# Attention scores in three steps instead of four, with zero-padded K pieces, and a gate value spread by TensorE

## Chip, cores, metric

One Trainium2 chip, one core. The metric is the device time of one execution in microseconds (us); smaller is better. Times are medians of several executions. The profile gives the start and length of nearly every instruction of one of them.

## The reference, cut to what matters

There are 8 sentences of 576 positions. Each goes through causal attention with 8 heads of width 64 and a forget gate that makes old keys count less; then each whole sentence goes through one of 8 experts, chosen by a gate.

```python
scores = (q @ k.T) / sqrt(64)
cum    = cumsum(log(clip(f, 1e-4, 1)))
scores = where(causal, -1e9, scores + cum[:, None] - cum[None, :])
x      = softmax(scores) @ v                     # 8 sentences x 576 x 512
e      = argmax(mean(x, over positions) @ w_gate)    # one expert per sentence
gate   = softmax(mean(x) @ w_gate)[e]
out    = gate * (relu(x @ w1[e]) @ w2[e])        # 512 -> 1024 -> 512
```

## The kernel before

Work comes in 16 groups (g0 to g15) of four heads, two per sentence, and 8 experts (b=0 to 7). A group is: transposes of q and k on DVE, score matmuls, exponentials on ACT, causal masks on GpSimd, products with V on TensorE ("PV"), normalisation on ACT and DVE. An expert is: gate, request for the weights W1 and W2, H (16 pieces of four matmuls), relu, O, eviction, store.

The score columns of a group were cut in four steps. Half a step is two heads, in a tile of two PSUM banks; there are two such tiles, so a step of four heads fills both, and the next step has to wait until the exponentials have read them.

```python
STEPS = (((0, 0, 448, 0),),                        # (K chunk, first q, last q, column)
         ((1, 128, 576, 0),),
         ((2, 256, 576, 0), (4, 512, 576, 320)),
         ((3, 384, 576, 0), (0, 448, 576, 192)))
...
def expo(g, s, halves):
    e = E[od.slot(("e", g))][s]
    for n in halves:
        nc.scalar.activation(e[:, 2*n:2*n+2, :], PS_S[...][:, :, 0:WIDTH[s]], AF.Exp, scale=0.125)
...
def gate6(op, b):                                  # one number to 128 partitions, by a transfer
    nc.sync.dma_start(GATE[i], ROW[i])
```

The order of the instructions on each engine is not written by hand. A small program in the kernel (`Order`) plays the run through once with assumed durations, picks at each moment the ready operation of the best priority, and emits it. After that the order is fixed: each engine works through its own list and waits at the head of the list, even where something later in it would be ready. Where it has nothing for TensorE, it emits filler matmuls that compute nothing. This matters below.

```python
HOP = 0.12                    # assumed time for an engine to see another one's result, us
...
st = od.add(f"S{tag}", "PE", {448: .41, 384: .37, 320: .31}[n], ..., after=..., takes=(("s", (g, s, x)),))
hm = od.add(f"H{b}{j}{half}", "PE", .49, ..., after=[ld if b else quarters[j // 2], g6])
om = od.add(f"O{b}{sb}a", "PE", us, ..., after=list(rel.values()) + ...)   # O waits for all eight h
```

The softmax here doesn't subtract the row's maximum and nothing guards it: scores larger than these inputs give would overflow.

Of the kernel before, what the change touches and what calls it, by code (L numbers as in the profile page):

```python
# [11 lines left out]
P = 128  # L12
# [12 lines left out]
STEPS = (((0, 0, 448, 0),),  # L25
         ((1, 128, 576, 0),),
         ((2, 256, 576, 0), (4, 512, 576, 320)),
         ((3, 384, 576, 0), (0, 448, 576, 192)))
WIDTH = (448, 448, 384, 320)

BLOCKS = ((0, 256, ((0, 0, 0, 256, 0), (1, 1, 128, 256, 0))),
          (256, 576, ((1, 1, 256, 576, 128), (0, 0, 256, 448, 256), (2, 2, 256, 576, 0),
                      (0, 3, 448, 576, 192), (3, 3, 384, 576, 0), (4, 2, 512, 576, 320))))

MAX_SPAN = 72.0

W_LOW, W_HIGH = 8.6e-17, 1.2e16
LN_SCALE = 2.0 ** -3
FILL = 60.0
# [6 lines left out]
LAG = 3  # L46
# [5 lines left out]
LOOK = {1: (0, 0, 0), 2: (0, 1, 2), 3: (1, 0, 2), 4: (1, 0, 2)}  # L52


class Op:
# [3 lines left out]
    def __init__(self, name, engines, us, fn, after=(), prio=0.0, takes=(), gives=(), lands=None, grain=None, runs=0, behind=()):  # L59
        self.name, self.us, self.fn, self.prio = name, us, fn, prio  # L60
        self.engines = engines if isinstance(engines, tuple) else (engines,)
        self.after, self.takes, self.gives, self.lands = list(after), takes, gives, lands
        self.end, self.grain, self.runs = None, grain, runs
        self.behind, self.issued = behind, None
        self.engine = None


class Order:
# [4 lines left out]
    def __init__(self, rings):  # L73
# [6 lines left out]
        self.filler, self.fill_until, self.spare = None, 0.0, 0  # L80
# [22 lines left out]
    def advance(self, now):  # L103


        while self.clock < now - 1e-9:
# [9 lines left out]
            for q in live:  # L116
                if q[0][1] < 1e-6:
                    op = q.pop(0)[3]
                    op.end = self.clock + 0.4
                    self.give(op)  # L120

# [17 lines left out]

    def run(self):  # L140
        left = list(self.ops)
        busy = dict.fromkeys(("PE", "ACT", "DVE", "POOL", "SP"), 0.0)
        now = 0.0
        busy["PE"] = 2.0
        while left:
# [5 lines left out]
            for e, until in busy.items():  # L151
# [4 lines left out]
                for op in left:  # L156
                    if e not in op.engines:
                        continue
                    ready = 0.0
                    for a in op.after:  # L160
                        if a.end is None:
                            ready = None
                            break
                        ready = max(ready, a.end + (0.0 if a.engine == e and a.lands is None else self.HOP))
                    for a in op.behind:
                        if a.issued is None:
                            ready = None
                        elif ready is not None:
                            ready = max(ready, a.issued)
                    if ready is None:  # L170
                        continue
# [13 lines left out]
            if best is None and self.filler is not None and now < self.fill_until and busy["PE"] <= now + 1e-9:  # L185
# [9 lines left out]
            if best is None:  # L195
                assert horizon is not None, (self.held, [o.name for o in left if all(a.end is not None for a in o.after)])
# [3 lines left out]
            op.engine = e  # L200
            for ring, key in op.takes:
# [4 lines left out]
                if ring in self.turn:  # L206
                    self.turn[ring].pop(0)
            if e == "PE" and self.mode(op) != self.last:
# [11 lines left out]
            left.remove(op)  # L220
# [5 lines left out]
def fast_path(ctx, tc, q, k, v, f, moe_w_gate, moe_w1, moe_w2, out, flag):  # L226
# [16 lines left out]
    KT = [const.tile([P, S], fp32, name=f"kt{i}") for i in range(RINGS["qt"])]  # L243
    VF = [const.tile([P, NCH, NH, D], fp32, name=f"vf{i}") for i in range(RINGS["vf"])]
    VB = [const.tile([P, NCH, 4, D], bf16, name=f"vb{i}") for i in range(RINGS["vb"])]
    E = [[const.tile([P, 4, WIDTH[s]], bf16, name=f"e{s}{i}") for s in range(4)] for i in range(RINGS["e"])]
# [13 lines left out]
    ROW = small("row", [1, P])  # L260
    seen_to = const.tile([P, 1], fp32, name="seen")[64:65, :]
# [5 lines left out]
    span = const.tile([NB * NH, 1], fp32, name="span")  # L267
    mxs = const.tile([1, NB * NH], fp32, name="mxs")
    mx8 = const.tile([1, 8], fp32, name="mx8f")
    WF = const.tile([P, NB, NCH, NH], fp32, name="WF")  # L270
    WB = const.tile([P, NB, NCH, NH], bf16, name="WB")
    wg = const.tile([P, 4, NE], fp32, name="wg")
    ident = const.tile([D, D], fp32, name="identf")
    still = const.tile([P, 512], bf16, name="still")

# [34 lines left out]
    def first(op):  # L310
        nc.scalar.preload_act_table_set("natural_log_exp_and_others")
        nc.sync.dma_start(F, f.rearrange("b h s -> (b h) s"))
        nc.vector.memset(still, 0.0)  # L313
        for t in VB:
            nc.vector.memset(t[0:64, 4, :, :], 0.0)
        nc.vector.memset(WF[0:64, :, 4, :], 0.0)

    loadf = od.add("F", "SP", 0.5, first, prio=-50, lands=0.5, grain=.1)
    idop = od.add("ident", "POOL", 0.8, lambda op: make_identity(nc, ident), prio=-1)
# [9 lines left out]
    last = [loadf]  # L329
    for b in range(NB):  # L330
        for c in range(10 if b < VQ else 5):
# [3 lines left out]
                                   takes=(("vf", b),) if c == 0 else (), lands=(1.4 if c5 < 4 else .7) / (2 if b < VQ else 1), grain=.022, runs=(64 if c5 < 4 else 32) // (2 if b < VQ else 1),  # L335
                                   behind=last if b < VQ else [loads_v[b, c - 1]] if c else [])
# [13 lines left out]
    def cum3(op):  # L350
        nc.vector.tensor_scalar_mul(mid, span, -0.5)
        nc.vector.tensor_tensor_scan(CUM, LOGF, LOGF, mid[:, 0:1], op0=ALU.add, op1=ALU.bypass)
# [13 lines left out]
    def cum6(op):  # L366
        pw = PS_W[od.slot(("bank", "cum"))]
        for w in (WF[:, :, 0:4, :], WF[64:P, :, 4, :]):
            nc.vector.tensor_scalar(w, w, W_LOW, W_HIGH, op0=ALU.max, op1=ALU.min)
        nc.vector.tensor_copy(WB.rearrange("p b c h -> p (b c h)"), WF.rearrange("p b c h -> p (b c h)"))  # L370
# [5 lines left out]
    c2 = od.add("cum2", "ACT", 0.68, cum2, after=[c1], prio=0.5)  # L376
    c3 = od.add("cum3", "DVE", 1.45, cum3, after=[c2], prio=2)
    c4 = od.add("cum4", "PE", 0.8, cum4, after=[c3, idop], prio=0, takes=(("bank", "cum"),))
    c5 = od.add("cum5", "ACT", .7, cum5, after=[c4], prio=0)
    c6 = od.add("cum6", "DVE", 0.9, cum6, after=[c5], prio=0, gives=(("bank", "cum"),))  # L380
# [3 lines left out]
    def to_t(g, j, lo=0, hi=4):  # L384
        raw = RAW[j][od.slot(("raw", g))][32 * lo:32 * hi].bitcast(fp32).rearrange("p (r w) -> p r w", w=32)
        dst = (QT, KT)[j][od.slot(("qt", g))][32 * lo:32 * hi].rearrange("p (t r) -> p r t", r=18)
        nc.vector.transpose(dst, raw)  # L387

    def banks_of(g, s, n):

        i = od.slot(("s", (g, s, n)))
        return [(2 * n + j, PS_S[i][:, j, :]) for j in range(2)]

    def step(g, s, halves):
        i = od.slot(("qt", g))
        kt, qt = KT[i].bitcast(bf16).rearrange("p (t r) -> p t r", r=2), QT[i].bitcast(bf16).rearrange("p (t r) -> p t r", r=2)
        for c, i0, i1, col in STEPS[s]:
            for r in range(2):
                for h, ps in [x for n in halves for x in banks_of(g, s, n)]:
                    nc.tensor.matmul(ps[:, col:col + i1 - i0], kt[32 * h:32 * h + 32, KLO[c]:KLO[c] + P, r],  # L400
                                     qt[32 * h:32 * h + 32, i0:i1, r], start=(r == 0), stop=(r == 1))

    def expo(g, s, halves):
        e = E[od.slot(("e", g))][s]
        for n in halves:
            nc.scalar.activation(e[:, 2 * n:2 * n + 2, :], PS_S[od.slot(("s", (g, s, n)))][:, :, 0:WIDTH[s]], AF.Exp, scale=0.125)  # L406

    def mask(g, s):
        e = E[od.slot(("e", g))][s]
        nc.gpsimd.affine_select(out=e[:, :, 0:128], in_=e[:, :, 0:128], pattern=[[0, 4], [1, 128]],  # L410
                                channel_multiplier=-1, base=0, compare_op=ALU.is_ge, fill=0.0)
        if s == 2:
            nc.gpsimd.affine_select(out=e[:, :, 320:384], in_=e[:, :, 320:384], pattern=[[0, 4], [1, 64]],
                                    channel_multiplier=-1, base=64, compare_op=ALU.is_ge, fill=0.0)
# [444 lines left out]
```

## Time and profile before

| | before |
|---|---|
| time, median | 251.07 us (250.03 to 252.89, three runs; a fourth came with the result) |
| TensorE (PE) busy | 229.7 us, 92% of the profiled span of 250.8 |
| ACT / GpSimd (POOL) / DVE busy | 71% / 51% / 46% |
| share of TensorE in the chain that ended last | 73% |
| first H matmul | 39.3 us |
| last matmul | 244.4 us |

The lines themselves, and the order in which they are read, are in the prediction.

To compare the kernels I use one account that the profile does not give directly. For each pair of successive matmuls in the trace I take the time from start to start and subtract a **price**: columns at 2.4 per ns (shared by four where four strips work side by side, by two in the 64-row O group), 2.5 ns for a matmul of the full array, and the 0.13 us that a change between row strips, column strips and the full array costs; all of these come out of this trace. What is left is a **gap**. From 40 us on, the kernel before has 185.4 us of price and 18.0 us of gaps. 17 of its 256 O matmuls have no record, though; at 0.216 us each their 3.7 us sit among the gaps, so 189.1 and 14.3 are the true sums. Its variants below whose records are complete but for one give 188 to 190 and 14 to 16.

### The profile page before, as it was taken

To read this page: it belongs to the slowest core of one execution; us is meant where nothing else is said; L and a number is where in the kernel's file an instruction comes from. 1 tells how busy PE (TensorE), PEld (TensorE's weight loads), DVE (VectorE), ACT (ScalarE), POOL (GpSimd) and SP (SyncE) were. 2 spreads that over 40 slices of the span, in tenths; PEclk is the share of its full clock that TensorE was granted. 3 is DMA by queue.
4 is the path that set the end of the run, shared out by engine and by line. 5 is a ranking of instruction groups with operands and counts; after the bars stand their busy time and mean duration, and the time that the engine had idled before them with its cause. 6 is when DMAs were issued, how large, how long until landed. Compare 5 with 4: busy or idle time off the path is not lost.

```text
span 250.8 us, 8039 instructions
## 1 busy us (share of the span) xinstructions
PE 229.7 (92%) x3304; PEld 146.2 (58%) x3325; DVE 115.4 (46%) x305; ACT 177.2 (71%) x313; POOL 127.0 (51%) x197
## 2 busy tenths in 40 slices
PE   6799997999889999799999999899998999999990
PEld 2333734674366846567458755586586656957840
DVE  3892882667533941278136942694146342200000
ACT  3466846897799968849779874896488787855820
POOL 6046739971995546714992649363822872300000
PEclk9657999999999999979999999999999999999996
DMA  6996849999999999990999999999993598299032
GB/s 119 221 221 118 146 73 180 201 207 212 177 220 212 215 204 226 297 213 8 173 219 213 277 218 215 254 227 209 227 278 76 82 232 216 36 212 256 29 121 75
DMA packets 59946, 45.84 MB, mean 183 GB/s; under 512 B 40896, under 2 KB 43968, under 8 KB 59904
## 3 DMA queue, kind: packets, MB, share of 16 engines
q0 software_dynamic: 14848, 26.22, 59.1%
q1 hardware_dynamic: 32576, 15.90, 25.1%
q10 hardware_dynamic: 12480, 3.15, 6.1%
q8 instruction: 28, 0.46, 0.7%
q14 instruction: 14, 0.11, 0.1%
HBM read 62.03 MB, written 9.44 MB: 285 GB/s over the span
## 4 chain that ended last, share of the span: by engine, by line
PE 73%; DMA 7%; issue 6%; POOL 6%; ACT 3%; DVE 2%; POOLq 1%; ACTq 0%; DVEq 0%
PE ps_w L595 24%; PE ps_w L612 20%; PE ps_s L400 12%; PE ps_w L439 11%; PE ps_w L615 3%; PE ps_w L680 3%; DMA out_dram<-otile 3%; DMA w1e<-in_moe_w_dram 2%; ACT e L406 2%; DMA rawq<-in_q_dram 2%; POOL e L410 2%; POOL vb L423 1%; DVE qt L387 1%; POOL rawk L281 1%; PE ps_w L548 1%
## 5 line engine op out<-in xcount | busy, mean ns | idle before, releaser
L406 ACT ACTIVATE e<-ps_s 128x896 bf16<-128x896 f32 (+2 forms) x128 | 100.2, 834 | 28.7 <-PE ps_s L400 27.9
L410 POOL TENSOR_SCALAR_AFFINE_SELECT e<-e 128x512 bf16<-128x512 bf16 x64 | 41.7, 656 | 69.0 <-ACT e L406 68.4
L595 PE MATMUL ps_w<-xT,w1e 128*128 128x288 bf16 x512 | 71.0, 292 | 3.4 <-DVE xT L459 1.9
L595 PEld LDWEIGHTS <-w1e 128*128 128x128 bf16 x512 | 60.5, 139 | 11.5 <-issue 4.9
L612 PE MATMUL ps_w<-w2e,h1T 128*128 128x512 bf16 x239 | 57.5, 380 | 1.9 <-issue 1.4
L400 PE MATMUL ps_s<-qt,kt 32*128 32x448 bf16 (+4 forms) x768 | 42.1, 289 | 5.6 <-ACT e L406 2.8
L459 DVE SCALAR_TENSOR_TENSOR xT<-ps_w,lr 128x256 bf16<-128x256 f32 (+1 forms) x64 | 26.8, 455 | 37.1 <-ACT lr L449 30.6
L605 ACT ACTIVATE h1T<-ps_w,gate_b 128x288 bf16<-128x288 f32 x77 | 37.4, 499 | 4.9 <-PE ps_w L595 4.7
L612 PEld LDWEIGHTS <-h1T 128*128 128x128 bf16 x256 | 22.8, 98 | 28.5 <-issue 3.6
L603 DVE TENSOR_SCALAR h1T<-ps_w,gate_b 128x288 bf16<-128x288 f32 x51 | 25.3, 505 | 28.6 <-PE ps_w L595 28.2
L400 PEld LDWEIGHTS <-kt 32*128 32x128 bf16 x768 | 17.6, 95 | 27.5 <-issue 21.5
L439 PE MATMUL ps_w<-e,vb 128*32 128x320 bf16 (+4 forms) x1024 | 29.4, 251 | 1.8 <-issue 1.5
L423 POOL TENSOR_TENSOR vb<-vf,WF 128x512 bf16<-128x512 f32 x29 | 30.5, 1053 | 0.3
L387 DVE STREAM_TRANSPOSE kt<-rawk 128x576 f32<-128x576 f32 (+1 forms) x17 | 21.3, 1252 | 19.4 <-DMA rawk<-in_k_dram 16.3
L624 ACT COPY otile<-ps_w 128x512 f32<-128x512 f32 (+1 forms) x25 | 14.0, 560 | 21.9 <-PE ps_w L612 20.9
L439 PEld LDWEIGHTS <-vb 128*32 128x32 bf16 x1024 | 21.3, 97 | 7.0 <-issue 4.7
L387 DVE STREAM_TRANSPOSE qt<-rawq 128x576 f32<-128x576 f32 (+1 forms) x17 | 21.1, 1244 | 0.6 <-DMA rawq<-in_q_dram 0.5
L680 PE MATMUL ps_w<-still 128*128 128x512 bf16 x51 | 17.4, 472 | 2.1 <-DVE still L313 1.4
L622 DVE COPY otile<-ps_w 128x512 f32<-128x512 f32 (+1 forms) x15 | 9.0, 599 | 21.2 <-PE ps_w L612 19.8
L439 PE MATMUL ps_w<-e,WB 128*32 128x192 bf16 (+4 forms) x512 | 17.3, 253 | 0.1
L576 POOL DMA_DIRECT2D w1e<-in_moe_w_dram x14 | 10.2, 731 | 13.1 <-DVE h1T L603 11.4
L444 ACT ACTIVATE lr<-ps_w 128x256 f32<-128x256 f32 (+1 forms) x31 | 12.7, 411 | 4.8 <-PE ps_w L439 4.5
(55 smaller groups left out, 129.4 us busy)
## 6 DMA issues: line engine op xcount, KB each, us to landing
w2e<-in_moe_w_dram POOLq DMA_DIRECT2D x8, 1024.0 KB, 14.2
out_dram<-otile SPq DMA_DIRECT2D x32, 256.0 KB, 7.4
w1e<-in_moe_w_dram POOLq DMA_DIRECT2D x14, 512.0 KB, 7.6
rawk<-in_k_dram POOLq DMA_DIRECT2D x15, 288.0 KB, 7.2
rawq<-in_q_dram POOLq DMA_DIRECT2D x15, 288.0 KB, 8.7
vf<-in_v_dram SPq DMA_DIRECT2D x12, 256.0 KB, 9.3
vf<-in_v_dram ACTq DMA_DIRECT2D x12, 256.0 KB, 12.2
vf<-in_v_dram SPq DMA_DIRECT2D x22, 128.0 KB, 6.0
```

What stands on the lines that cost most here:

```text
L387: nc.vector.transpose(dst, raw)
L400: nc.tensor.matmul(ps[:, col:col + i1 - i0], kt[32 * h:32 * h + 32, KLO[c]:KLO[c] + P, r], qt[32 * h:32 * h + 32, i0:i1, r], start=(r == 0 ...
L406: nc.scalar.activation(e[:, 2 * n:2 * n + 2, :], PS_S[od.slot(("s", (g, s, n)))][:, :, 0:WIDTH[s]], AF.Exp, scale=0.125)
L410: nc.gpsimd.affine_select(out=e[:, :, 0:128], in_=e[:, :, 0:128], pattern=[[0, 4], [1, 128]], channel_multiplier=-1, base=0, compare_op=AL ...
L423: eng.tensor_tensor(vb[:, c, :, :], vf[:, c, h, :], WF[:, b, c, h].unsqueeze(3).to_broadcast([P, 2, 4, D]), op=ALU.mult)
L439: nc.tensor.matmul(ps[32 * h:32 * h + 32, lo - i0:hi - i0], lhs, e[s][:, h, col:col + hi - lo], start=(n == 0), stop=(n == len(parts) - 1) ...
L459: nc.vector.scalar_tensor_tensor(XT[od.slot(("x", b))][:, mm, i0:i1], ps[:, 0:i1 - i0], 1.0 if (g, blk) in ON_DVE else LN_SCALE, LR[od.slo ...
L595: nc.tensor.matmul(ps[:, 0:288], lhs, xT[:, m, 288 * half:288 * half + 288], start=(m == 0), stop=(m == 3))
L603: nc.vector.tensor_scalar(dst, ps[:, 0:288], g[:, 0:1], 0.0, op0=ALU.mult, op1=ALU.max)
L605: nc.scalar.activation(dst, ps[:, 0:288], AF.Relu, scale=g[:, 0:1])
L612: nc.tensor.matmul(ps, h[:, j, P * sb:P * sb + P], r, start=(j == 0), stop=(j == 7))
L680: od.filler = lambda i: nc.tensor.matmul(PS_W[i], still[:, 0:P], still[:, 0:512])
```

## The change

The intent is to spend less TensorE time: one score step and its mode changes less per group, no transfer in the gate's path, and O matmuls that start as soon as half of h is there. Step 2 now holds chunk 2, the upper half of chunk 3 and chunk 4. For that, K gets two extra pieces of which one half is zero, so that a full-height matmul adds a half chunk. The diff, cut to its core:

```diff
-STEPS = (((0, 0, 448, 0),), ((1, 128, 576, 0),),
-         ((2, 256, 576, 0), (4, 512, 576, 320)), ((3, 384, 576, 0), (0, 448, 576, 192)))
+STEPS = (((0, 0, 512, 0),), ((1, 128, 576, 0), (0, 512, 576, 448)),
+         ((2, 256, 576, 0), (None, 384, 512, 320), (3, 448, 576, 384)))
...
+if c is None:                                   # the padded pieces
+    for n in range(2):
+        nc.tensor.matmul(ps[:, col:col+64], kt[row, S+64*n:S+64*n+P, r], qt[row, i0+128*n:i0+128*n+64, r], ...)
...
-nc.sync.dma_start(GATE[i], ROW[i])
+nc.tensor.matmul(ps[:, 0:1], ROW[i], one)       # gate spread by PE
+nc.vector.tensor_copy(GATE[i], ps[:, 0:1])      # (an own piece of the plan)
...
-om = ... after=list(rel.values()) + outs[-1:] + [ld2]
+om = ... after=[x for (j, _), x in rel.items() if j < 4] + outs[-1:] + [ld2]
...
-FILL = 60.0                                     # fillers until 60 us
+FILL = (28.0, 60.0)                             # none before the planned 28 us
-LAG = 3                                         # q, k of group g asked for after V of group g-3 is scaled
+LAG = 2
```

Not shown: a second half-chunk of V to scale, masks that DVE may take (all of groups 2 and 3), V loads that wait for a DVE mark, and other assumed durations in the plan.

## The prediction

> **What bounds the kernel now.** I read the page first (engine shares, slices, chain), then the time-ordered chain, then the timeline of some score steps, then the groups split by shape and the ten-microsecond windows.
>
> ```profile
> PE 229.7 (92%) x3304; PEld 146.2 (58%) x3325; DVE 115.4 (46%) x305; ACT 177.2 (71%) x313; POOL 127.0 (51%) x197
> PE   6799997999889999799999999899998999999990
> PEclk9657999999999999979999999999999999999996
> PE 73%; DMA 7%; issue 6%; POOL 6%; ACT 3%; DVE 2%; POOLq 1%; ACTq 0%; DVEq 0%
> ```
>
> TensorE is busy 92% of the span and carries 73% of the chain, so after the beginning a microsecond of TensorE work is worth about a microsecond. But the digits are dense from the first slices only because of filler matmuls (L680: x51, 17.4 us busy), which compute nothing. The beginning is a latency chain:
>
> ```profile
> 18.06 0.65 PE ps_s L400 x8
> 18.70 2.25 PE ps_w L680 x5
> 20.95 0.76 PE ps_s L400 x6
> 21.74 0.92 ACT e L406
> ...
> 36.19 0.48 POOL w1e L580
> 37.59 6.23 DMA w1e<-in_moe_w_dram
> 43.86 1.40 PE ps_w L595 x10
> ```
>
> Five fillers stand in front of the scores of the second group of four heads (g1) for 2.25 us; the exponentials follow, then masks, PV, the gate, and only then can the expert's W1 be asked for (first request at 35.48 us in the timeline). Dense TensorE work starts when it lands, at 43.86. I count the first 44 us as one account and the rest as another. Up to 44 us TensorE had done real work of about 13.7 us: three score groups, two PV groups, 28 H matmuls, at the warm prices below. So some 30 us of the span are start-up, about 6 us are the last store (last matmul 244.4, end 250.8), and the rest is TensorE work with about 11 us of gaps.
>
> The price of a score step, from start to next start in the timeline:
>
> ```profile
> 45.19 0.58 PE L400 MATMUL ps_s<-qt,kt 32*128 32x448 bf16 x8
> 45.70 2.63 PE L595 MATMUL ps_w<-xT,w1e 128*128 128x288 bf16 x20
> ...
> 50.68 0.54 PE L400 MATMUL ps_s<-qt,kt 32*128 32x320 bf16 x16
> 51.15 1.31 PE L439 MATMUL ps_w<-e,vb 128*32 128x320 bf16 x48
> ...
> 53.97 0.46 PE L400 MATMUL ps_s<-qt,kt 32*128 32x192 bf16 x16
> 54.37 0.35 PE L439 MATMUL ps_w<-e,WB 128*32 128x256 bf16 x8
> ```
>
> 448, 384 and 320 columns cost 0.51, 0.45 to 0.47 and 0.40 us. 64 columns fewer save 0.053 us: two passes at 2.4 columns per ns. What is left is a constant 0.13 us per step, whether it holds 8 matmuls or 16. A group of four steps costs 0.505+0.505+0.453+0.395=1.86 us.
>
> ACT, by shape:
>
> ```profile
> L406 ACT ACTIVATE e<-ps_s 128x896 bf16<-128x896 f32 x64 | 55.2, 913 | 18.3 <-PE ps_s L400 18.0
> L406 ACT ACTIVATE e<-ps_s 128x640 bf16<-128x640 f32 x32 | 20.9, 701 | 3.9 <-PE ps_s L400 3.6 <-DMA vf<-in_v_dram 0.2
> ```
>
> That is 0.83 ns per element and 0.17 us fixed.
>
> **What the Trainium skill says.** "TensorEngine Tiling (Array Packing)", Key Properties, says that changing the tiling mode drains the array. The trace agrees in kind: the 0.13 us that each score step costs beyond its columns appears at every change between row strips, column strips and the full array. "TensorE: Matmul & The Clock Gate", What's actually happening, says the array starts at half clock and is released by activity over a window of about 3.4 us. The trace agrees on the two clocks: the window 10 to 20 us has granted clock 0.50 although TensorE was busy 9.67 of 10 us there, so filling did not buy a warm clock in time. "ScalarE: Activation LUTs", Rules for kernel authors, budgets about 0.3 us and 0.83 ns per element for an activation; the slope agrees, the fixed part here is 0.17, and I use that.
>
> **The change part by part.**
>
> *Scores in three steps.* Columns streamed per group: before 448+448+384+320=1600; after 512+512+(320+64+64+128=576)=1600. Only one 0.13 us constant per group goes: 16 x 0.13 = 2.1 us less. Against it, the zero-padded pieces are two 64-column matmuls in succession on the same row strip, where all others alternate over four strips. If they fully serialize, eight take about five 27 ns slots instead of two: 0.08 us per pass, 0.17 us per group, 2.7 us in all. I take half, 1.3. Net -0.8 us.
>
> *Exponentials.* Before 4x0.913+2x0.807+2x0.701=6.67 us per group as the means of single instructions; in a row they start every 0.81, 0.70 and 0.60 us, 5.84 us. After six of 1024 elements, about 0.92 apart, 5.5 us. Some 5 us of ACT in all, off the path except at the start.
>
> *PV.* Columns stay at 1600; 36 matmuls instead of 32 for each product of a group. Four of 64 columns already take only 27 ns here, so no cost.
>
> *Masks and V.* The e3 mask goes, the second part of e2 goes to DVE for nearly all groups (built order), and groups 2 and 3 have all theirs on DVE. GpSimd's 656 ns masks fall from 64 to about 43 (-14 us), its 418 ns ones go (-7), 14 more V scalings at 0.61 come (+8.5), and seven copies of K. About 10 us less GpSimd; DVE gets these, and 14 more evictions of H, some 15 us, at 46% busy. No direct effect.
>
> *Gate by TensorE.* Eight DMAs go; the one early in the trace took 2.0 us from issue to landing. They were beside the W1 load, whose 512 KB pieces take a median of 7.6 us, so nothing is gained on the path. Eight small fp32 matmuls are added; the four gate matmuls together cost 0.28 us, so I take 0.15 each: +1.2 us.
>
> *O after four of h.* In the last two experts the x16 group of O starts 1.15 us before the next, while at 54.97 it took 1.00: a wait of 0.16 us for the last eviction, in most of 8 experts. Sum -1.0 us.
>
> *The start (not named in the change's title, but in the diff).* No fillers before the planned 28 us (51 or more become 13), V loads start after a DVE mark, behind the first q and k; the flag arithmetic moves off the front; no transpose stands between the gate matmul and its maximum. I walk the chain. V's DMAs begin about 1.4 us later, so first q should land about 1 us earlier than 6.74: first scores near 7 instead of 8.04. The scan and its exponential follow 1 to 1.5 us earlier. g1's raw q and k are asked for about 1.4 us later (they wait behind the first V), so its transposes finish about where they did, 16.4. But its first scores then start there instead of at 20.88, as neither fillers nor late exponentials stand before. At the cold clock the three double steps and the PV between them take about 8 us, so the last exponential of g1 ends near 25.4 instead of 29.3. From there to the last norm took 3.0 us and keeps that. The gate's maximum, held 0.6 us by a transpose (32.41 to 33.66), comes 0.6 us sooner after it. W1 is requested near 31.1 instead of 35.5: -4.4 us. In the built order PV of groups 2 and 3 stands between the first H pieces, where TensorE used to wait for W1 quarters (about 1 us idle at 39.7, 0.5 at 43.3): -1.0.
>
> *Gaps later.* Two stretches stand out:
>
> ```profile
> 60.00:70.00 10.00, 8.35 (x100) 3.50 (x96) 4.75 (x14) 7.58 (x12) 6.72 (x11) 1.00 0.90 183
> 100.00:110.00 10.00, 8.13 (x143) 5.98 (x145) 3.99 (x12) 5.66 (x11) 5.78 (x9) 0.84 1.12 271
> ```
>
> The first is a pile-up of scores on the exponentials while masks wait in GpSimd's queue; the second is DVE's queue held by a K transpose whose transfer is late (6.0 us), followed by a spell of half clock. Fewer steps and less GpSimd work help the first; the second depends on when transfers are issued, and q and k are now asked for one group later, which may hurt. I take -1.5 us.
>
> Sum: -0.8 +1.2 -1.0 -4.4 -1.0 -1.5 = -7.5 us. 251.07-7.5 = 243.5 us.
>
> **Rivals.**
> (1) The start is bound by transfers, not by fillers and exponentials. The DMA share is 1.14 in 10 to 20 us, and the bytes are the same. Then the request for W1 moves by 1 to 2 us only and the time is about 247. For it: the saturated transfers; against it: the fillers lie on the chain at 18.70, and g1's first transpose follows other DVE work at once.
> (2) The clock stays cold longer without fillers, so the PV of g1 and the first H pieces run at half speed. That costs 2 to 3 us: about 246. For it: in the trace the clock rose only after long filling; against it: the later fillers (13) remain.
> (3) Transfers become the bound in the middle: their share is over 1 in most windows, and a shorter lead of q and k loads makes DVE's queue block oftener. Then the start's gain is given back: about 249 or 250.
> (4) GpSimd's queue no longer holds the masks at all, and most of the 11 us of gaps close: about 237.
>
> **Range and chances.** The start is most of it, -2 to -6; gaps -5 to +3; prices of TensorE work within 2. Together 243.5, with 237.5 to 248 eight times in ten. The 2% border is 246.05 and needs about 5 us; the start alone nearly gives it. Faster 0.78, within 0.20, slower 0.02.
>
> **What would show it.** The W1 request near 31 us and dense H work near 36 to 39; score steps of 0.56, 0.56 and 0.61 to 0.78 us; each gate spread at most 0.15 us; the x16 group of O at 1.00 us; TensorE's work after the start shorter by about 1 us and the gaps by 1 to 2. If W1 is requested after 33 us, the walk through the start is wrong; if the total is right but the start is not, the gaps were mis-sized; if the padded step takes over 0.8 us, strip order is the fault.

## The result

| | before | changed |
|---|---|---|
| time, median | 250.55 us (249.38 to 252.89) | 258.92 us (257.70 to 259.64) |
| ratio of fast runs | | 1.032 (1.023 to 1.041): slower |
| first H matmul | 39.3 us | 35.5 us |
| gate matmuls of b=2 | 82.8 us | 91.8 us |
| last matmul | 244.4 us | 251.0 us |

A ratio is the mean time of one kernel's fast runs over that of the other's fast runs of the same rounds, so not quite the ratio of the medians. All runs of both here were fast.

The kernel is 8 us slower; the prediction was 243.5. First the page of the changed kernel (busy time, slices, granted clock, chain by engine):

```profile
PE 225.1 (88%) x3619; PEld 148.6 (58%) x3619; DVE 140.0 (55%) x365; ACT 166.4 (65%) x268; POOL 123.0 (48%) x189
PE   0889888699999987699799999999989898999991
PEclk9999999999999997999999999999999999999999
PE 63%; DMA 18%; DVE 5%; issue 5%; ACT 3%; POOL 2%; POOLq 1%; ACTq 0%; DVEq 0%
```

TensorE has less to do, 225.1 us instead of 229.7, and carries less of the chain, 63% instead of 73%. Transfers took the difference: 18% instead of 7%. The digits 7 and 6 in the middle are the 16th and 17th slice, 96 to 109 us. The chain in order of time shows which transfers (start, length, what):

```profile
19.21 1.92 PE ps_s L454 x16
23.98 3.30 PE ps_w L495 x45
38.09 11.88 DMA rawk<-in_k_dram
...
56.20 12.38 DMA w1e<-in_moe_w_dram
...
94.63 10.77 DMA w1e<-in_moe_w_dram
```

Neither a filler nor a wait for W1 of the first expert is in it now. Instead it holds a load of K for 11.9 us and W1 of the second and third expert for 12.4 and 10.8 us. That the beginning really was shortened is in the timeline of the changed kernel, where the first request for W1 starts at 31.76 us (before: 35.48):

```profile
31.76 4.90 POOL L656 DMA_DIRECT2D w1e<-in_moe_w_dram  x7 [4.32 <-DVE row L627]
```

The score steps, in TensorE's timeline (start, length, what), and ACT's group of exponentials by shape:

```profile
85.49 0.63 PE L454 MATMUL ps_s<-qt,kt 32*128 32x512 bf16 x8
86.05 0.71 PE L495 MATMUL ps_w<-e,WB 128*32 128x320 bf16 x28
...
89.39 0.64 PE L454 MATMUL ps_s<-qt,kt 32*128 32x448 bf16 x16
89.95 1.90 PE L703 MATMUL ps_w<-w2e,h1T 128*128 128x512 bf16 x8
```

```profile
L459 ACT ACTIVATE e<-ps_s 128x1024 bf16<-128x1024 f32 x96 | 93.2, 1020 | 23.2 <-PE ps_s L454 22.2
```

From start to next start the first two steps take 0.56 us each; the third, with the padded pieces, took 0.63 where nothing held it (as at 60.7 and 71.1 us). A group costs 1.75 instead of 1.86 us. ACT's exponentials fell from 100.2 to 93.2 us. So the parts did what they were meant to. The loss is in TensorE's gaps. Ten-microsecond windows (busy PE, PEld, DVE, ACT, POOL; clock; DMA share; GB/s), first of the kernel before, then of the changed one:

```profile
90.00:100.00 10.00, 9.95 (x85) 5.26 (x85) 1.60 (x3) 7.19 (x12) 5.26 (x8) 1.00 1.16 214
120.00:130.00 10.00, 9.79 (x166) 4.94 (x164) 2.42 (x9) 7.10 (x12) 9.81 (x15) 1.00 1.10 190
```

```profile
60.00:70.00 10.00, 9.54 (x96) 4.71 (x95) 2.52 (x5) 7.29 (x9) 1.97 (x4) 1.00 1.12 237
90.00:100.00 10.00, 7.30 (x110) 3.52 (x110) 5.47 (x13) 7.11 (x10) 7.92 (x12) 0.92 1.04 220
100.00:110.00 10.00, 7.53 (x240) 5.01 (x232) 2.77 (x12) 8.07 (x15) 7.07 (x11) 0.91 1.13 210
120.00:130.00 10.00, 8.03 (x189) 4.87 (x186) 3.17 (x11) 7.96 (x12) 9.00 (x14) 1.00 1.12 224
```

The pile-up at 60 to 70 us is gone, as I had hoped (9.54 busy, before 8.35). But in 90 to 100 us TensorE stands still for 2.7 us where before it lost 0.05. The account of gaps from 40 us on, in us, for four of the kernels (two are experiments told below):

```
window        before   f1_b_hop16   changed   g4_a_all
40 to 60        1.1        0.8         5.0       5.2
60 to 80        4.4        3.1         0.7       0.3
80 to 100       0.6        0.4         6.6       5.7
100 to 120      4.5        6.4         4.8       4.5
120 to 140      0.9        1.6         3.5       2.7
140 to 200      5.2        2.2         3.0       2.3
200 to 240      1.4        0.7         4.2       0.6
sum            18.0       15.2        27.7      21.3     (before: 3.7 of it missing records)
price         185.4      189.8       182.7     182.1     (before: 3.7 more)
```

From 40 us on the price fell by 6.4 us (189.1 to 182.7; part of that is work that now lies before 40 us) and the gaps grew by 13.4 us (14.3 to 27.7). Together +7.0, which is the 6.6 us by which the last matmul is later, within 0.4. The question is what the 13 us of gaps are waits for. The longest stretch, in TensorE's timeline of the changed kernel (brackets: idle before it, and what ended the idle time):

```profile
94.19 0.38 PE L631 MATMUL ps_w<-one,row 1*128 1x1 f32 x2 [0.46 <-DVE row L627]
94.84 0.40 PE L454 MATMUL ps_s<-qt,kt 32*128 32x512 bf16 x2 [0.27 <-ACT e L459]
95.75 0.62 PE L454 MATMUL ps_s<-qt,kt 32*128 32x512 bf16 x6 [0.51 <-ACT e L459]
97.28 0.37 PE L454 MATMUL ps_s<-qt,kt 32*128 32x448 bf16 x2 [0.90 <-ACT e L459]
...
103.20 0.34 PE L686 MATMUL ps_w<-xT,w1e 128*128 128x288 bf16 x1
105.44 0.59 PE L686 MATMUL ps_w<-xT,w1e 128*128 128x288 bf16 x3 [1.90 <-DMA w1e<-in_moe_w_dram]
```

Three kinds of waits follow each other: the gate spread holds the queue until DVE has its row, the score steps stand behind exponentials of 1024 elements, and H stands behind W1. Four suspects come from here: the gate, the exponentials, the weights, and the masks and V work (the added V scaling on GpSimd ended when PV went on at 128.7 us, and was taken for what it waited for; the next lines speak against that).

There is a fourth kind, and no experiment was aimed at it. Some pauses of TensorE carry no wait in the profile; they are marked "issue":

```profile
46.99 0.51 PE L495 MATMUL ps_w<-e,vb 128*32 128x256 bf16 x15 [1.94 <-issue]
128.71 0.46 PE L495 MATMUL ps_w<-e,vb 128*32 128x320 bf16 x18 [1.37 <-issue]
```

A third is at 216.30 us. The three, 5.0 us of gaps together, fall inside a PV product that has already begun. Count TensorE's records from the start of the trace (matmuls, weight loads, and its sequencer's own): work resumes at number 1217, 3777 and 6593, each time 193 past a multiple of 256. And 1.3 to 1.5 us before each resumption a packet of 16 KB has landed on queue q8, which the profile calls "instruction" (the first from 44.6 to 45.5 us). The 20 kept traces hold 56 such pauses of 0.3 us or more after 40 us. Every one ends 1.2 to 1.6 us after such a landing, against 12 of the 217 other gaps of that size, and 54 of them at 193 to 195 past a multiple of 256; the other two are in the trace of before, which misses records.

So TensorE very probably waited for its own next instructions there. These pauses are 5.7 us in the changed kernel and 1.9 in before, that is 3.8 of the 13.4 us by which the gaps grew. In the seven kernels of this study with four-step scores they are 0 to 2.3 us, in the thirteen with three steps 1.8 to 7.7. No run varied them on purpose: why there are more with three steps is open.

### The profile page after: what moved, and what is told of

Its sections match the earlier page's. It is cut to its first block, busy times and chain, and to the rows that moved or that the text cites. A ratio compares the mean times of both kernels' runs of the same rounds, so it can differ in the third digit from the quotient of the medians.

```text
span 256.7 us, 8624 instructions
## 1 busy us (share of the span) xinstructions
PE 225.1 (88%) x3619; PEld 148.6 (58%) x3619; DVE 140.0 (55%) x365; ACT 166.4 (65%) x268; POOL 123.0 (48%) x189
## 4 chain that ended last, share of the span: by engine, by line
PE 63%; DMA 18%; DVE 5%; issue 5%; ACT 3%; POOL 2%; POOLq 1%; ACTq 0%; DVEq 0%
PE ps_w L686 23%; PE ps_w L703 18%; PE ps_w L495 10%; DMA w1e<-in_moe_w_dram 9%; PE ps_s L454 8%; DMA rawk<-in_k_dram 5%; PE ps_w L706 3%; DMA rawq<-in_q_dram 2%; ACT e L459 2%; DMA vf<-in_v_dram 2%; POOL w1e L656 1%; DVE xT L515 1%; DVE qt L431 1%; DVE row L627 1%; PE ps_w L612 1%
## 5 line engine op out<-in xcount | busy, mean ns | idle before, releaser
L459 ACT ACTIVATE e<-ps_s 128x1024 bf16<-128x1024 f32 x96 | 93.2, 1020 | 23.2 <-PE ps_s L454 22.2
L703 PE MATMUL ps_w<-w2e,h1T 128*128 128x512 bf16 x256 | 59.7, 380 | 0.4 <-DVE xT L515 0.3
L454 PE MATMUL ps_s<-qt,kt 32*128 32x512 bf16 (+4 forms) x640 | 42.7, 312 | 13.7 <-DVE mid L391 7.4
L467 POOL TENSOR_SCALAR_AFFINE_SELECT e<-e 128x512 bf16<-128x512 bf16 x43 | 28.3, 662 | 50.3 <-ACT e L459 50.3
L694 DVE TENSOR_SCALAR h1T<-ps_w,gate_b 128x288 bf16<-128x288 f32 x65 | 33.0, 516 | 30.1 <-PE ps_w L686 29.3
L696 ACT ACTIVATE h1T<-ps_w,gate_b 128x288 bf16<-128x288 f32 x63 | 31.2, 502 | 25.1 <-PE ps_w L686 24.8
L495 PE MATMUL ps_w<-e,vb 128*32 128x64 bf16 (+3 forms) x1152 | 32.1, 252 | 4.9 <-issue 4.3
L642 POOL DMA_DIRECT2D w1e<-in_moe_w_dram x14 | 10.2, 733 | 24.3 <-DVE kt L431 11.9
L713 DVE COPY otile<-ps_w 128x512 f32<-128x512 f32 (+1 forms) x14 | 8.6, 615 | 22.5 <-PE ps_w L703 19.9
L495 PE MATMUL ps_w<-e,WB 128*32 128x64 bf16 (+3 forms) x576 | 19.0, 258 | 0.4 <-POOL e L467 0.3
L483 POOL TENSOR_TENSOR vb<-vf,WF 64x256 bf16<-64x256 f32 x28 | 17.4, 621 | 2.2
L495 PEld LDWEIGHTS <-WB 128*32 128x32 bf16 x576 | 11.7, 102 | 8.6 <-issue 6.2
```

What stands on the lines that cost most here:

```text
L454: nc.tensor.matmul(ps[:, col:col + i1 - i0], kt[row, KLO[c]:KLO[c] + P, r], qt[row, i0:i1, r], start=(r == 0), stop=(r == 1))
L459: nc.scalar.activation(e[:, lo:lo + 2, :], banks, AF.Exp, scale=0.125)
L467: nc.gpsimd.affine_select(out=x, in_=x, pattern=[[0, 4], [1, P]], channel_multiplier=-1, base=0, compare_op=ALU.is_ge, fill=0.0)
L483: eng.tensor_tensor(vb[rows, d, :, :], vf[rows, c, h, :], WF[rows, b, c, h].unsqueeze(2).to_broadcast([64, 4, D]), op=ALU.mult)
L495: nc.tensor.matmul(ps[32 * h:32 * h + 32, lo - i0:hi - i0], lhs, e[s][:, h, col:col + hi - lo], start=(n == 0), stop=(n == len(parts) - 1) ...
L694: nc.vector.tensor_scalar(dst, ps[:, 0:288], g[:, 0:1], 0.0, op0=ALU.mult, op1=ALU.max)
```

## The experiments

18 kernels ran. "Changed" and "before" are the two kernels above; before ran in the same rounds each time (medians 251.2 to 252.1 us). Unless said otherwise the results were correct. Runs in a slow state are left out of the ratios.

### One part undone, or one part alone

**e1_lag3**: the lag and its look-ahead entry as before.

```diff
-LAG = 2
+LAG = 3
-LOOK = {1: (0, 0, 0), 2: (0, 1, 2), 3: (1, 0, 2)}
+LOOK = {1: (0, 0, 0), 2: (0, 1, 2), 3: (1, 0, 2), 4: (1, 0, 2)}
```

> The changed kernel, with the q and k loads issued as early as before again (one group earlier, and the fourth look back). Theory A (the gaps in the middle come from q and k asked for too late: scores of group 6 start 8.5 us later than before although the start gained 4 us): 250 to 253 us. Theory B (the gaps come from an order of instructions fixed beforehand from planned durations that the chip does not keep, so one part undone gives back only its own price): 256 to 260 us.

Measured: 262.35 us, ratio 1.039 (1.032 to 1.046). Asking for q and k earlier does not help. The theory that the shorter lag is the loss falls.

**e2_gate_dma**: the gate by a transfer again, order kept.

```diff
-nc.tensor.matmul(ps[:, 0:1], ROW[i], one)
+return
-nc.vector.tensor_copy(GATE[i], ps[:, 0:1])
+nc.sync.dma_start(GATE[i], ROW[i])
```

> The changed kernel with every instruction in the same place, only the gate is spread by a DMA again in place of the TensorE matmul and its eviction. Theory C (the spread matmul stands in TensorE's in-order queue and holds it while it waits for the row: gaps of 0.9 and 1.2 us at it, and 8 x 0.31 us of its own): 254 to 256 us. Theories A and B: only its own price, 2 us, 256 to 257.5 us. If the DMA's landing is late for the evictions of H, the time stays or rises.

Measured: 255.77 us, ratio 1.009 (1.002 to 1.017; one of four runs was slow). The change by the median is 3.2 us, by the ratios (1.032 to 1.009, of 251) 5.6 us. So the gate spread costs some 3 to 6 us. Eight spreads of 0.31 us, start to start with their mode changes, are 2.5 us; the rest is what the queue waits for the row, as at 94.19 above.

**e3_o_all**: O after all eight h again, in the plan.

```diff
-after=[x for (j, _), x in rel.items() if j < 4] + outs[-1:] + [ld2]
+after=list(rel.values()) + outs[-1:] + [ld2]
```

> The changed kernel with O planned after all eight of h again. Theory A and C: a wait of 0.16 us in each of 8 experts comes back, 258 to 260 us. Theory B: the order shifts as a whole, so it may land anywhere from 254 to 262 us.

Measured: 257.71 us, ratio 1.023 (1.016 to 1.030; one of four runs was slow). O after four brings nothing here; undoing it is, if anything, better.

**e4_fill0**: fillers from the start, as before (the plan then also drops its allowance for the cold clock).

```diff
-FILL = (28.0, 60.0)
+FILL = (0.0, 60.0)
```

> The changed kernel with fillers from the start again (and so no planned cold price). If the start's gain (first W1 request 3.7 us earlier) is real and carries to the end, this loses it: 260 to 263 us. If the start does not matter because the transfers of the middle bound the time anyway (as much data has moved at 110 us in both kernels), the time stays within 1 us: 258 to 260.

Measured: 261.12 us, ratio 1.033 (1.025 to 1.041). The median is 2.2 us up, the ratio hardly (1.032). The time lies in the range set for a start whose gain carries to the end, but the ratio does not; at most about 2 us of the 3.8 arrive, and even that is not clear of the scatter.

**e5_b_three**: the kernel before with the three-step scores alone (padded K, masks, second V half), nothing else.

```diff
-STEPS = four steps
+STEPS = three steps, KT with 192 more columns, VB and WB with one more chunk
+again(...), the mask of the padded part on DVE or GpSimd, the second V half-chunk
```

> The kernel before with the three-step scores alone (padded K pieces, seven PV parts, the second mask of the last step on DVE or GpSimd, the extra half scaling of V); gate by DMA, O after eight, loads, fillers and planned durations as before. If the three steps are the loss (scores bunched in double steps wait 0.86 us for exponentials; more V scaling on GpSimd): 256 to 259 us. If they are what the column count says and the loss lies elsewhere: 249 to 252 us.

Measured: 263.32 us, ratio 1.045 (1.036 to 1.055). Its gaps from 40 us on are 29.0 us, 9.5 of them between score steps (before 2.3, changed 6.6). Of these 9.5, 3.0 are two pauses without a recorded wait (64.06 and 116.95 us) and 5.3 are six waits for exponentials; in all the pauses without a wait are 7.7 us here. Its first H is at 41.5 us, later than before. The new scores alone open the gaps.

**e6_a_four**: the changed kernel with the four-step scores of before, everything else kept.

```diff
-STEPS = three steps and all that belongs to them
+STEPS = four steps of before
```

> The changed kernel with the four-step scores of before and everything else of the change. If the three steps are the loss: 250 to 253 us. If the rest is (gate on TensorE, load order, planned durations, start): 257 to 261 us.

Measured: 265.08 us, ratio 1.055 (1.046 to 1.065). It looks as if the other half were guilty too, but the profile says otherwise. TensorE's timeline of this run near the end:

```profile
234.61 0.34 PE L670 MATMUL ps_w<-xT,w1e 128*128 128x288 bf16 x1 [4.06 <-DMA w1e<-in_moe_w_dram]
238.16 1.18 PE L670 MATMUL ps_w<-xT,w1e 128*128 128x288 bf16 x4 [3.21 <-DMA w1e<-in_moe_w_dram]
```

In this order the attention of the last sentence came so late that nothing was left to do while the last expert's weights travelled: 7.3 us idle. So this run is inconclusive about the rest of the change.

### Is it the order as such?

By now every kernel with a fresh order was slower than before. The plan had promised 243.7 us for the changed kernel (that is the end that the order-drawing program reports; for before 247.9), and the chip took 15 us longer. Was before's order just a lucky one?

**f1_b_hop16** and **f2_a_hop11**: only the assumed hop in the plan differs, so that about 100 of some 380 pieces of TensorE work change place.

```diff
-HOP = 0.12
+HOP = 0.16        # f1, in the kernel before
+HOP = 0.11        # f2, in the changed kernel
```

> The kernel before with nothing of the change in it. One number that only the program which fixes the order reads is altered: the assumed time for an engine to see another engine's result, 0.12 us -> 0.16 us. Instructions, sizes, loads and buffers are the same; about 100 of the 388 planned pieces of TensorE work stand in another place. The planned end is 247.2 us (unaltered: 247.9). Theory B (the time of before, 251, belongs to one lucky or selected order, and any fresh order ends 13 to 19 us after its plan, as the changed kernel and four of my variants did): 256 to 263 us. Theory C (before is short because of what it does, and the three-step scores, the two-turn lag, the gate spread and the rest cost the 8 us): 250 to 253 us.

> The changed kernel with the same number altered the other way, 0.12 -> 0.11 us; about 97 of 378 planned pieces of TensorE work move; the planned end is 244.5 us (unaltered: 243.7). Theory B: anywhere in 253 to 264 us, since the order decides and the plan does not tell which order is good. Theory C: within 1% of the changed kernel, 256.5 to 261.5 us.

Measured: f1 253.34 us, ratio 1.005 (0.999 to 1.010); f2 259.35 us, ratio 1.030 (1.023 to 1.037). My theory B fell: a redrawn order of before is as good as before, a redrawn order of the changed kernel as slow as it. Gaps from 40 us on: 15.2 and 28.0 us. In f2 they lie elsewhere than in the changed kernel (8.8 of them at 200 to 220 us), but their sum is the same. So, as far as one redraw of each can tell, the content makes the gaps and the order only places them.

**f3_b_ofour**: before, with O after four alone.

```diff
-om = ... after=list(rel.values()) + outs[-1:] + [ld2]
-on = ... after=[om]
+om = ... after=[x for (j, _), x in rel.items() if j < 4] + outs[-1:] + [ld2]
+on = ... after=[om] + list(rel.values())
```

> The kernel before with the third part of the change alone: O begins when four of the eight h are there. Only 24 of 388 planned pieces of TensorE work move; planned end 247.1 us (before 247.9). My prediction put this part at -1.0 us: 250 to 251 us. Theory B, with few pieces moved: between 249 and 256 us. If it is over 253 us, a small re-draw is already enough to lose the tuned order.

Measured: 252.33 us, ratio 1.004 (0.996 to 1.013). Nothing, as in e3_o_all.

**f4_a_gate**: changed, gate by a transfer, order drawn anew.

```diff
-g6 = od.add(f"g6{b}", "PE", .15, ...)    # and g7 on DVE
+g7 = od.add(f"g6{b}", "SP", .5, ..., lands=.2)
```

> The changed kernel with the gate spread by a small transfer as in before, and the order drawn up anew for it (in the earlier run e2_gate_dma the order was kept). Planned end 250.1 us, 6.4 us later than the plan of the changed kernel. If the plan were a guide to the chip this would be 265 us; if the removed 3 us of the gate spread decide, 255 us as in e2_gate_dma; theory B: anywhere in 253 to 264 us.

Measured: 264.99 us median; two of its four runs were slow (the fast ones 261.15 and 262.90), so no ratio is taken. It is not as good as e2_gate_dma, which has the same instructions in another order. The order does matter within the family, by several us; only it does not explain the step from before to changed.

**g1_b_nofill**: before in its own order, without the fillers before 28 us.

```diff
-self.filler(ok[0][1])
+if now >= 28.0:
+    self.filler(ok[0][1])
```

> The kernel before in its own order, with the filler matmuls that the plan places before 28 us left out (the changed kernel has none there either); nothing else differs. In the trace of before the clock is at 0.50 from 8 to 20 us while fillers run, in the changed kernel it is at 1.00 there and the first H starts 3.8 us sooner. If the fillers are what halves the clock and the start is worth its 3.8 us, the time is 247 to 248.5 us, below both kernels. If the rest of the start's gain came from the three-step scores or other loads, 250 to 252 us. If the fillers did warm the clock, later than 252 us.

Measured: 252.71 us, ratio 1.001 (0.994 to 1.009). A window of before, then the same of this run (third figure from the end in each: the granted clock):

```profile
12.00:16.00 4.00, 3.80 (x25) 1.33 (x23) 3.82 (x9) 2.49 (x5) 0.00 (x0) 0.50 1.24 236
```

```profile
12.00:16.00 4.00, 3.20 (x24) 1.60 (x23) 3.83 (x9) 3.48 (x6) 1.78 (x3) 1.00 1.24 235
```

The first PV starts at 17.3 us instead of 21.6, so the fillers did hold up TensorE. But the gate's matmuls come at 30.9 instead of 32.5 and the first H at 39.2 instead of 39.3: the lead is lost again. One reason stands in the matmuls' own times. Without fillers TensorE ran at half speed for longer: four PV matmuls of 320 columns side by side took 0.26 us up to 28.2 us and 0.13 from 29.0 on, while in before they took 0.13 already at 24.2. The granted clock of 1.00 does not tell this. So the fillers did bring full speed sooner, and held up TensorE meanwhile; the fillers alone are not the start's gain.

### What TensorE waits for

The next kernels remove a suspected wait in the fixed order. All were built to give wrong results on purpose (g2_a_exp still passed the comparison with the reference, as stale exponentials of an earlier group stand in for the missing ones).

**e7_b_light** and **e8_a_light**: from the fourth expert on only a quarter of the weights is loaded, in before and in changed.

```diff
+n = 256 if b > 2 else FH
-dma_start(W1[w]...[:, q], src[:, q])
+dma_start(W1[w]...[:, q, :, 0:n], src[:, q, :, 0:n])
+n = 1024 if b > 2 else 4096                    # W2 likewise
```

> WRONG RESULT ON PURPOSE. The kernel before, every instruction in its place, but the experts' weights of batch elements 3 to 7 loaded to a quarter only (the rest of the buffer keeps old values). If transfers bound the middle: 241 to 246 us. If TensorE and the fixed order do: 248 to 250 us.

> WRONG RESULT ON PURPOSE. The changed kernel with the same cut of weights. If the changed kernel is slower because its transfers crowd (Theory T): it falls as far as to the light kernel before or below it, 240 to 247 us. If it is slower because of its order and its waits between engines (Theory B): it stays about 6 to 8 us above the light kernel before, 252 to 257 us.

Measured: before 251.22 us, ratio 0.998 (0.992 to 1.005); changed 254.05 us, ratio 1.011 (1.005 to 1.017). The kernel before shows no wait for these transfers that is clear of the noise. The changed one gains about 5 us (1.032 to 1.011, of 251). Its profile does not say that TensorE waited for the cut weights: TensorE's larger waits for W1 from 40 us on are 2.8 us in both, here all of it for the third expert, whose load this run leaves whole. What fell are the pauses without a recorded wait, from 5.7 to 1.8 us. That fewer bytes let the instructions come in time is a guess; no run tests it.

**g2_a_exp**: exponentials of 256 instead of 1024 elements from group 4 on.

```diff
-activation(e[:, lo:lo+2, :], banks, AF.Exp, ...)
+w = 128 if g > 3 else 512
+activation(e[:, lo:lo+2, 0:w], banks[:, :, 0:w], AF.Exp, ...)
```

> Wrong result on purpose: the changed kernel in its own order, with each exponential cut from 1024 to 256 elements a partition from group 4 on. Theory X (TensorE's gaps of 0.86 and 1.23 us between score steps, at 94 to 99, 108.7 and 125.6 us of the changed trace, wait for the longer exponentials behind two score tiles): 252 to 255 us. If ScalarE's length is not what is waited for: 257 to 260 us.

Measured: 254.64 us, ratio 1.013 (1.004 to 1.021). The gaps between score steps fall from 6.6 to 1.2 us. The prediction had put the exponentials "off the path except at the start"; they are on it. But look at the stretch from before in TensorE's timeline of this run:

```profile
98.23 1.34 PE L496 MATMUL ps_w<-e,vb 128*32 128x320 bf16 x56
101.15 0.34 PE L687 MATMUL ps_w<-xT,w1e 128*128 128x288 bf16 x1 [1.58 <-DMA w1e<-in_moe_w_dram]
103.32 0.94 PE L687 MATMUL ps_w<-xT,w1e 128*128 128x288 bf16 x3 [1.82 <-DMA w1e<-in_moe_w_dram]
```

TensorE came there sooner, and now waits 3.4 us for W1 instead of 1.9.

**g3_a_pool**: masks of one column, and no second V half, from group 4 on.

```diff
+if g > 3:
+    eng.tensor_copy(x[:, :, 0:1], x[:, :, 0:1]); return
-for rows, c, d in (first half, second half):
+for rows, c, d in (first half, second half)[0:1 if g > 3 else 2]:
```

> Wrong result on purpose: the changed kernel in its own order, with the causal masks cut to one column and the added second half-chunk scaling of V left out from group 4 on. Theory M (PV's gaps of 1.2 to 1.6 us at 128.7 and 216.3 us wait for that added work on GpSimd and for the masks): 254 to 256.5 us. If it is beside the path: 257.5 to 260 us.

Measured: 257.97 us, ratio 1.025 (1.017 to 1.032). At most 2 us. At the PV of 128.7 us the GpSimd work that ended last is gone, yet PV resumes only 0.8 us sooner (127.95), after a pause of 1.5 us, 1.2 us after a packet on q8 landed: it was one of the pauses without a recorded wait, and so was the one at 216.3. Theory M was aimed at the wrong wait.

**g4_a_all**: the four cuts together (exponentials, masks and V, late weights, gate).

> Wrong result on purpose: the two cuts above, the weights of the last five experts loaded to a quarter and the gate spread by a transfer, all together, in the changed kernel's own order. If the waits for these four things are the whole loss, little of it is left and the time is 245 to 248 us, near the 243.5 us that I predicted for a kernel whose gaps do not grow. If over 251 us, something else still holds TensorE.

**h2_b_cut**: its control, the same cuts in before (there is no second V half to cut, and the gate is a transfer anyway).

> Wrong result on purpose, the control for g4_a_all: the kernel before in its own order with the same cuts (exponentials to 256 elements and masks to one column from group 4 on, weights of the last five experts to a quarter; its gate is spread by a transfer anyway). g4_a_all fell 7 us below the changed kernel. If those waits are the change's own, before loses little by the same cuts: 249 to 252 us. If it falls to 245 us or less, such waits are in both kernels and the cuts say nothing of the change.

Measured: g4 251.75 us, ratio 0.998 (0.991 to 1.004); h2 248.44 us, ratio 0.996 (0.985 to 1.006), the medians 2.8 us apart. With the four cuts, the changed kernel is level with the uncut before, 3.4% below its own ratio; before itself hardly gains by the same cuts, 0.4% by ratio and 1.1% by medians. Net of the control the cuts take away 3.0 of the 3.2% by ratios, but only 4.4 of the 8.4 us by medians, so they hold between half and nearly all of the loss. Part of that is work and not waiting: eight gate spreads are 2.5 us of TensorE's time. The pauses without a recorded wait stay at 5.7 us in g4. Alone, the four cuts had taken off 2.2, 2.1, 1.9 and 0.7%, which is 6.9% in sum. So they overlap: where one wait is removed, another with nearly the same end takes its place.

**h1_a_light1**: of the weights of every expert but the first, half of W1 and a quarter of W2 are loaded, and the matmuls read that part.

```diff
-dma_start(W1[w]...[:, q], src[:, q])
+dma_start(W1[w]...[:, q, 0:1], src[:, q, 0:1])
-lhs = w1[:, 2 * (m % 2) + m // 2, j::8]
+lhs = w1[:, m // 2, j::8]                      # W2 likewise
```

> Wrong result on purpose: the changed kernel in its own order; of the weights of every expert but the first, half of W1 and a quarter of W2 are loaded, and the matmuls read the loaded part (e8_a_light did this from the fourth expert on and left the loads of the second and third whole). Theory W: the gaps of about 11 us between 80 and 120 us, which no cut so far has moved (g4_a_all kept 10 of them), hang on the weights of the third expert, requested at 93.9 and landed at 105.4 us. Then the time falls another 3 to 6 us below the 254.0 us of e8_a_light, to 248 to 251 us. If it stays at 253 to 255 us, the wait for these weights is beside the path.

Measured: 255.94 us, ratio 1.023 (1.014 to 1.031). Theory W missed. The wait for W1 at 105 us did go, but the stretch in TensorE's timeline of this run says why that gave nothing:

```profile
95.77 0.62 PE L454 MATMUL ps_s<-qt,kt 32*128 32x512 bf16 x6 [0.51 <-ACT e L459]
97.30 0.37 PE L454 MATMUL ps_s<-qt,kt 32*128 32x448 bf16 x2 [0.90 <-ACT e L459]
...
103.18 0.71 PE L686 MATMUL ps_w<-xT,w1e 128*128 128x288 bf16 x4
```

The waits for exponentials stay, and H starts at 103.2 us, the same as in the changed kernel. Cutting the exponentials leaves the wait for W1, cutting W1 leaves the exponentials, and either way the gaps from 80 to 120 us are 10 us (changed: 11.4). Removing both here was not run: g4_a_all still loads the third expert's W1 whole. That it would close the stretch is argued, not shown. This run also loads fewer bytes than e8_a_light and is not faster, so the value of the transfers is uncertain, 2 to 5 us.

No kernel of this study beats before by more than the scatter, unless it gives a wrong result.

## Why the prediction was wrong, by its own steps

- **"After the beginning a microsecond of TensorE work is worth about a microsecond."** This premise failed. TensorE's work got shorter, and the last matmul came 6.6 us later. A chain share of 73% says how much of the chain lies on TensorE as the kernel stands; it does not say how near the next engine is. In the changed kernel the share was 63% at once.
- **The start, -4.4.** Right at its own place: W1 was requested at 31.76 us (31.1 predicted), the first H came 3.8 us sooner. But this lead was spent between 40 and 60 us, where the gaps are 5.0 instead of 1.1 us. At 46.99 us PV stood for 2.2 us without a recorded wait, at 53.5 the gate's matmuls for 0.7, and two score steps waited 1.4 us for exponentials. e4_fill0 and g1_b_nofill agree: a start that is sooner on TensorE hardly arrives at the end. Part of rival (1) and (3).
- **PV between the first H pieces, -1.0.** Not seen: the gaps from 40 to 60 us stand where it should have shown.
- **Scores in three steps, -0.8.** The price was mis-sized in the good direction: the padded pieces cost 0.02 us per step beyond their columns and mode change (0.63 against 0.61), where I had taken 1.3 us in all for half serialised strips. What I had not asked is what a step waits for. e5_b_three shows 9.5 us of gaps between score steps, 7 more than before, 3.0 of them without a recorded wait.
- **Exponentials, "off the path except at the start".** Wrong: g2_a_exp gives 1.9% when they are shortened. ACT does less in sum (166.4 instead of 177.2 us), but what counts is how long TensorE stands at a step with no other work in front of it: 0.86 and 1.23 us at a time. (The 0.3 us of the Trainium skill, "ScalarE: Activation LUTs", Rules for kernel authors, that the prediction set beside its 0.17 is for a bias given as a pointer operand; the trace names none for these exponentials, `e<-ps_s`, so the two figures do not contradict each other.)
- **Masks and V, "no direct effect".** Nearly right: at most 2 us in g3_a_pool. GpSimd got 4.0 us less busy (127.0 to 123.0) where I had said 10.
- **Gate by TensorE, +1.2.** Wrong by a factor of at least 2.5: 3 to 6 us, with 0.31 us each instead of 0.15, and the head of TensorE's queue waits for DVE's row. A transfer had done that without holding an engine.
- **O after four of h, -1.0.** The wait that I saw did go (the x16 group takes 1.00 us), but f3_b_ofour and e3_o_all show no time from it.
- **Gaps later, -1.5.** The step that failed most: the gaps from 40 us on grew by 13.4 us. The 60 to 70 us pile-up closed as told, and others opened. Taking gaps over 0.3 us by what ended them, from before to changed: exponentials 4.0 to 6.5 us, W1 0.7 to 2.8, the gate's row 0 to 1.7, no recorded wait 1.9 to 5.7. The last of these the prediction did not think of.
- **Rivals.** (3) had the direction, "transfers become the bound in the middle", and e8_a_light shows that the bytes matter, by what path is not shown, but I stopped it at 249 or 250. (2), a cold clock without fillers, came true in part: the PV of g1 ran at half speed until 26.6 us (0.26 us for four of 320 columns), but W1 was asked for at 31.76 us all the same, and g1_b_nofill's time shows no loss. (4) did not happen. No rival had several engines' waits side by side.

What stays open: why the changed content needs 25 to 30 us of gaps in every order tried, when each single cut removes 1 to 5 us. Shown is that the four cuts together hold between half and nearly all of the loss against before, that they cover one another, and that about 10 us between 80 and 120 us (before 5.1) and 5 us between 40 and 60 us (before 1.1) outlive them all. Of these 5 us, 2.9 in g4_a_all are one pause without a recorded wait. The kernels with three steps have more of these pauses; what brings them was not tested.

## What to carry to other kernels

When an engine is at 92%, shortening its work is worth what it says only if the other engines' results come sooner too; ask for each piece that you shorten what it will wait for next. Look too for pauses in which the profile names no wait: here they made up 5.7 of 27.7 us of gaps, and two of them were first put down to the work that happened to end beside them. If several waits have nearly the same end, removing one shows little in the time, so remove them together, with the same cuts in the kernel before as a control, ahead of calling any of them harmless. And where an order is drawn up beforehand, redraw it in both kernels before blaming it: two runs settled that here.

## What the Trainium skill lacked or had wrong

- "TensorE: Matmul & The Clock Gate", What's actually happening, gives a busy window of about 3.4 us for the release of the clock. In before TensorE was busy 11.6 of the 12 us from 8 to 20 us, and filler matmuls of 512 columns still took 0.43 us at 19.9 us, twice the 0.216 that they took from 23.4 on. In g1_b_nofill, busy 14.5 of the 16 us from 8 to 24, half speed lasted until 28.2 us. The release took longer than the page's window in both. The granted clock read 0.50 in the first and 1.00 in the second, so the times of the matmuls themselves have to be looked at.
- "TensorEngine Tiling (Array Packing)", Key Properties, says that a mode change drains the array, without a figure. Here it is 0.13 us. No page has the two short matmuls in succession on one row strip: the padded pieces cost 0.02 us per step beyond the price of their columns and mode change.
- No page has a single value spread over 128 partitions by a one-row fp32 matmul: 0.31 us from start to start with its mode changes, and a wait at the head of the queue on top.
